# Keys' tiles that first hold x and the weights, and the first group's maxima among the projections

## The chip, the cores and the metric

The kernel runs on one core of one Trainium2 chip. The metric is the device time of one execution in microseconds (us); the time before is the median of three runs, 1368.82 us (1365.33 to 1370.16). A trace belongs to one profiled execution, which took 1366.65 us in all; the recorded span, from its first to its last instruction, is 1364.9 us.

## The reference, cut to what matters

Two independent computations, side by side in the output. A is a state-space convolution of u (2048 positions, 448 channels, 256 states); B is softmax attention with 16 heads of 28 on x (2048 x 448).

```python
qkv = (x @ wqkv).reshape(B, S, 3, H, Dh)      # q, k, v
scores = jnp.einsum("bhqd,bhkd->bhqk", q, k) * scale
p = softmax(scores, axis=-1)
o = jnp.einsum("bhqk,bhkd->bhqd", p, v)
b = o.transpose(...).reshape(B, S, D) @ wo

P = jnp.exp((A * dt[:, None])[:, :, None] * pos)       # pos = 0 .. L-1
K = 2.0 * jnp.einsum("dn,dnl->dl", C, P).real
y = irfft(rfft(u_t, 2 * L) * rfft(K, 2 * L))[:L] + u * D_skip
```

The softmax subtracts each query's maximum. What this kernel subtracts is a maximum over partly combined scores (below).

## The kernel before, in words

**Two phases.** The first phase ("p", from line 205) projects x to q, k and v and builds the *seeds* of the convolution's kernel K. The second ("a", from line 848) is a loop of 256 steps: 4 groups of 4 heads, 4 quarters of 512 queries (a pair of group and quarter is a *unit* u, 16 in all), 16 key tiles of 128. In it, work of the convolution is put between the attention's instructions by deques with due steps (`k_due`, `u_due`, `m_due`). In the second phase every instruction is kept in program order on its engine (`KEPT["a"]`); in the first none is, and the framework orders what is ready, earlier lines first.

**The first phase in stages.** `work` is a list of 48 jobs: for each quarter c of x, eight `qk_proj` (k and q of four groups) and four `v_proj`. Each job is 12 matmuls into one of three PSUM tiles, and an evacuation one job later: ACT writes the high part `th`, DVE the low part `tl` (two buffers of each), and SP writes both to DRAM (`k_d`, `q_d`; v goes through two staging tiles `vst` to `v_d`). The first job of a quarter also runs `transposes(c)`, the second loads the next quarter's x. For the first two quarters a k job also makes the difference of two halves of the keys and writes it to `kd_d`. In the last quarter the v jobs come before the q and k jobs.

The other strand is `seeds(o)`, eight of them, each a list of 13 steps on DVE, POOL and ACT, the steps of seed o at stages 4o to 4o + 12. The last two (`put_g`, `put_e`) write to DRAM. The scratch of `places()` is one of three `qhat` buffers. The loop over the 41 stages (line 515) runs, for stage t, as many jobs as are due (48 in the first 37 stages), then that stage's seed steps.

**What the change touches.** x lies in `y_p` (three half quarters, `xn`), v's weights in `y_p` (`vh`, `vl`), those of q and k in `w_p` (`wh`, `wl`). At stage 37 these pools close (`wst.close()`), and in the same memory `kd_p` (key differences, and the scratch `rl`) and `k0_p` (the four key tiles of a group, 128 x 2048 each, for even groups) are opened. Then SP is given `load_q(0)`, for each of four j `load_kd(0, j)` and `load_k(0, j)`, `load_q(1)` and four `load_v`. The keys of odd groups are in `kq_p`, a pool of the second phase. `load_k` reads one key tile in four DMAs.

**Maxima.** `max_mm(u, i, kc)` is one of 64 pieces of a unit's maxima: a matmul of 128 queries against 512 keys, and

- kc 0: against the key differences; ACT takes the Relu into `rl`;
- kc 1: against half of the keys of the first two quarters; DVE adds `rl` and reduces, in one instruction, and reads the result;
- kc 2 and 3: against the third and fourth quarter of the keys; DVE reduces.

So a step i needs DVE three times, and all four quarters of the keys. Unit 0's 16 steps follow the last stage, over five PSUM tiles (two `pt`, three `pm`). Then `max_join` reduces once more (`m<-mx` in the trace), `max_end` transposes, `max_put` writes the result into two rows of q's tile. The maxima of unit 1 and later run inside the loop, ahead of the scores by 16 key tiles and three (`LEAD`); three steps of unit 1 come just before the loop. After `sst.close()` the memory of the seeds goes to `kq_p` and `g_p`.

In the trace all engine instructions have the line of one helper (L73), so groups are told by tile names: `pm<-xh,wh` a projection of q or k, `pm<-vh,xh` one of v, `pt<-ident,xn` a transpose of x, `kdif`, `khat`, `qhat` a maximum, `pss` a score, `p` its exponential, `sg`, `tri`, `px`, `gz`, `x_e` the seeds (which also use `qhat` as scratch).

Of the kernel before, what the change touches and what calls it, by code (L numbers as in the profile page):

```python
# [1 line left out]

# [37 lines left out]
PS = 1  # L40
SGB, XB, XL = 2, 5, 4
K0, KP, KD, UP = 0, 3.5, 5, 3

N1 = 32
N2 = 64
# [43 lines left out]
def body(ctx, tc, a, out):  # L89
# [37 lines left out]

    q_p = pool(att, "q_p", side="right")
    v_p = pool(att, "v_p", side="right")

    def mm32(o, w, x_, start, stop, at=0):

# [4 lines left out]

    kt_g, kd_g, q_u, m_u, mh_u, o_u, rl_u = {}, {}, {}, {}, {}, {}, {}

    def load_k(g, j, p):  # L140
        t = p.tile([128, L], F32R, name="khat", bufs=HG)
        for r in range(4):
            nc.sync.dma_start(t[32 * r:32 * r + 32, :].bitcast(F32), k_d[g][r % 2, 32 * j:32 * j + 32, :])
        kt_g.setdefault(g, []).append(t)

    v_g = {}

# [4 lines left out]
    kd_p = [None]  # L152

    def load_kd(g, j):
        kd_g[g, j] = t = kd_p[0].tile([128, CQ], F32R, name=f"kdif{j}")
# [10 lines left out]
    def max_mm(u, i, kc, ps=w_tile):  # L166

        if i == 0 and kc == 0:
            m_u[u] = q_p.tile([128, HG, 4, 3], F32, name="mx", bufs=2)
        j, t = divmod(i, 4)  # L170
        pm = ps()
        q, kt = q_u[u][:, j, t * 128:(t + 1) * 128], kt_g[u // NQ][j]
        mx = m_u[u][:, j, t, max(kc - 1, 0):max(kc - 1, 0) + 1]
        if kc == 0:
            nc.tensor.matmul(pm, q, kd_g[u // NQ, j], start=True, stop=True)
            rl_u[u, i] = kd_p[0].tile([128, CQ], F32, name="rl", bufs=2)
# [26 lines left out]


    with ExitStack() as st:
        sst, xst, wst = ExitStack(), ExitStack(), ExitStack()
        t_p = pool(sst, "t_p")
        s_p = pool(sst, "s_p")
        x_p = pool(xst, "x_p")
        y_p = pool(wst, "y_p", side="right")  # L210
        w_p = pool(wst, "w_p", side="right")
# [6 lines left out]

        def load_x(c):
            xs = x[c * CQ:(c + 1) * CQ, :].rearrange("(t p) d -> p t d", p=128)  # L220
            for h in range(2):
                xns[c, h] = y_p.tile([128, 2, D], F32, name="xn", bufs=3)
                nc.sync.dma_start(xns[c, h], xs[:, 2 * h:2 * h + 2, :])

        load_x(0)
        wh = w_p.tile([CK, 2, NCK, H, 32], F32R, name="wh")
        wl = w_p.tile([CK, 2, NCK, H, 32], F32R, name="wl")
        vh = y_p.tile([CK, NCK, D], F32R, name="vh")
        vl = y_p.tile([CK, NCK, D], F32R, name="vl")
        for w in (wh, wl):  # L230
            nc.gpsimd.memset(w[:, :, :, :, DH:].bitcast(F32), 0.0)
        vst = [x_p.tile([128, H, 32], F32, name=f"vst{i}") for i in range(2)]
# [34 lines left out]
        for k in range(NCK):  # L267
            for s in (1, 0):
                src = wns[k][:, s, :].rearrange("p (h e) -> p h e", e=DH)
                nc.scalar.activation(wh[:, s, k, :, :DH], src, AF.Copy)  # L270
                nc.vector.tensor_tensor(wl[:, s, k, :, :DH], src, wh[:, s, k, :, :DH].bitcast(F32), ALU.subtract)
# [158 lines left out]
        def transposes(c):  # L430
            for k in range(NCK):
                pt = ps_t.tile([128, CQ], F32, name="pt")[:CK]
                for t in range(4):
                    nc.tensor.transpose(pt[:, t * 128:(t + 1) * 128], xns[c, t // 2][:, t % 2, k * CK:(k + 1) * CK], ident)
                xh[k] = x_p.tile([CK, CQ], F32R, name="xh", bufs=XB)
                xl[k] = x_p.tile([CK, CQ], F32R, name="xl", bufs=XL)
                nc.scalar.activation(xh[k], pt, AF.Copy)
                nc.vector.tensor_tensor(xl[k], pt, xh[k].bitcast(F32), ALU.subtract)

        def qk_proj(c, s, g):  # L440
            pp = w_tile()
            hs = slice(HG * g, HG * g + HG)
            n = 0
            for k in range(NCK):
                for w_, x_ in ((wh, xh), (wl, xh), (wh, xl)):
                    nc.tensor.matmul(pp, w_[:, s, k, hs, :].rearrange("p h e -> p (h e)"), x_[k],
                                     start=n == 0, stop=n == 3 * NCK - 1)
                    n += 1

            def evac():  # L450
                th = x_p.tile([128, CQ], F32R, name="th", bufs=2)
                tl = x_p.tile([128, CQ], F32R, name="tl", bufs=2)
                if s == 1:
                    nc.scalar.activation(th, pp, AF.Identity, bias=kones)
                    nc.vector.scalar_tensor_tensor(tl, pp, kones, th.bitcast(F32), op0=ALU.add, op1=ALU.subtract)
                else:
                    nc.scalar.activation(th, pp, AF.Copy)
                    nc.vector.tensor_tensor(tl, pp, th.bitcast(F32), ALU.subtract)
                if s == 1 and c < 2:
                    HC = CQ // 2  # L460
                    kb = y_p.tile([128, HC], F32, name="kb")
                    dh = y_p.tile([128, HC], F32R, name="dh")
                    dl = y_p.tile([128, HC], F32R, name="dl")
# [26 lines left out]
        for c in range(NQ):  # L490
            jobs = [lambda c=c, s=s, g=g: qk_proj(c, s, g) for g in range(G) for s in (1, 0)]
            v_jobs = [lambda c=c, t=t: v_proj(c, t) for t in range(4)]
            jobs = v_jobs + jobs if c == NQ - 1 else jobs + v_jobs
            jobs[0] = (lambda c, f: lambda: (transposes(c), f())[1])(c, jobs[0])
            if c + 1 < NQ:
                jobs[1] = (lambda c, f: lambda: (load_x(c + 1), f())[1])(c, jobs[1])
# [10 lines left out]
        def project():  # L507
# [4 lines left out]
            if e:  # L512
                pend.append(e)

        for t in range(n_stage):
            while work and n_work - len(work) < n_work * (t + 1) / PW:
                project()
            for f in slots[t]:
                f()
            if t + 1 == PW:  # L520
                project()
                wst.close()
                kd_p[0] = pool(att, "kd_p", side="right")
                k0_p = pool(k0_st, "k0_p", side="right")
                load_q(0)
                for j in range(HG):
                    load_kd(0, j)
# [24 lines left out]
    k_pools = [k0_p, kq_p]  # L552

    late = [False]

# [296 lines left out]
        for kc in range(4):  # L852
            max_mm(1, i, kc)

    import collections
# [124 lines left out]
    for s in range(NS):  # L980
# [18 lines left out]
        if sm < NS and sm % (NQ * NK) == 0 and sm:  # L999
            load_kd(sm // (NQ * NK), HG - 1)  # L1000
        if kt % 4 == 1 and u % NQ == 1 and u // NQ + 1 < G:
            load_k(u // NQ + 1, kt // 4, k_pools[(u // NQ + 1) % 2])
        if kt == 2:
            if u + 2 < NU:
                load_q(u + 2)
# [97 lines left out]
```

## Time and profile before

| | us |
|---|---|
| median of three runs | 1368.82 |
| profiled execution, in all | 1366.65 |
| its span | 1364.9 |
| PE busy | 1243.5 (91%) |
| DVE busy | 980.3 (72%) |
| ACT busy | 968.6 (71%) |
| POOL busy | 831.0 (61%) |
| mean granted clock of TensorE | 0.975 |
| moved by DMA | 205.37 MB, 150 GB/s over the span |

The profile's page gives the span in 40 slices; a digit is the busy share of an engine in tenths. Matmuls are pipelined: a projection's matmul is 0.4 us long, and the next begins 0.23 us after it. A view by windows gives the busy time of each engine between two times, with the granted clock and the DMA engines' share. The chain of waits follows the instruction that ended last back to what released it.

### The profile page before, as it was taken

What the parts mean: (1) busy time and instruction counts of PE and PEld (TensorE: products, weight loads), DVE (VectorE), ACT (ScalarE), POOL (GpSimd) and SP (SyncE); (2) the same over time, 40 slices, a digit from 0 to 9 for tenths busy, and PEclk for the clock granted to TensorE, in tenths of its full rate; (3) what the DMA queues carried; (4) which work ended last, traced back from release to release, by engine and by line L of the source; (5) the groups of instructions that cost most, each with busy time, mean ns of one, the idle gap of its engine ahead of it and who ended that gap; (6) DMA issues with size and microseconds to landing.
All of it is one profiled execution on the core that took longest, in us unless ns stands there. A gap on an engine that the chain in (4) does not pass through costs nothing.

```text
span 1364.9 us, 33230 instructions
## 1 busy us (share of the span) xinstructions
PE 1243.5 (91%) x12625; PEld 707.2 (52%) x12625; DVE 980.3 (72%) x2138; ACT 968.6 (71%) x2069; POOL 831.0 (61%) x705
## 2 busy tenths in 40 slices
PE   6978784799999999999999999999998999998997
PEld 4866662355555555555555555555555545544433
DVE  5778765877777777777788888887887766857311
ACT  4867662488888888888888888878786665655553
POOL 3576661187877877878878988888896111202221
PEclk9988896999999999999999999999999999999999
DMA  6775679726675546378533233632324544636476
GB/s 194 241 243 193 219 263 246 208 62 140 160 168 119 131 125 155 109 205 209 161 96 88 64 72 78 148 86 66 77 66 139 181 123 154 208 109 205 138 192 178
DMA packets 200729, 205.37 MB, mean 150 GB/s; under 512 B 96632, under 2 KB 159160, under 8 KB 198520
## 3 DMA queue, kind: packets, MB, share of 16 engines
q1 hardware_dynamic: 200568, 203.23, 53.5%
q8 instruction: 100, 1.64, 0.5%
q14 instruction: 61, 0.50, 0.1%
HBM read 120.73 MB, written 82.18 MB: 149 GB/s over the span
## 4 chain that ended last, share of the span: by engine, by line
PE 58%; DVE 16%; ACT 11%; POOL 5%; DMA 5%; issue 3%; SPq 0%; ACTq 0%; DVEq 0%; POOLq 0%
PE pm L73 34%; PE po L73 13%; PE pss L73 12%; ACT p L73 6%; DVE mx L73 3%; POOL qhat L73 3%; DVE g L73 2%; ACT rl L73 2%; DVE p L73 2%; DMA khat<-k 2%; DVE tri L73 1%; DVE pr L73 1%; DVE px L73 1%; POOL x_e L73 1%; DVE sg L73 1%
## 5 line engine op out<-in xcount | busy, mean ns | idle before, releaser
L73 ACT ACTIVATE p<-pss 128x512 f32<-128x512 f32 x1024 | 565.3, 608 | 137.0 <-PE pss L73 128.4
L73 PE MATMUL pss<-qhat,khat 128*128 128x512 f32 x1024 | 402.2, 399 | 3.5 <-ACT p L73 3.4
L73 DVE TENSOR_REDUCE mx<-pm 128x1 f32<-128x512 f32 x500 | 321.4, 683 | 104.6 <-PE pm L73 103.4
L73 PE MATMUL pm<-khat,qhat 128*128 128x512 f32 x749 | 329.7, 443 | 41.5 <-DVE mx L73 36.1
L73 POOL TENSOR_TENSOR e<-e,sdb 128x256 f32<-128x256 f32 x168 | 201.9, 1202 | 166.0 <-ACT e L73 157.0
L73 PE MATMUL po<-p,v 128*32 128x512 f32 x2048 | 271.8, 598 | 0.0
L73 POOL TENSOR_TENSOR e<-e,eu 128x256 f32<-128x256 f32 x168 | 248.5, 1479 | 13.2
L73 PEld LDWEIGHTS pm<-khat,qhat 128*128 128x128 f32 x749 | 141.0, 189 | 217.7 <-DVE mx L73 83.4
L73 PEld LDWEIGHTS pss<-qhat,khat 128*128 128x128 f32 x1024 | 190.6, 188 | 45.9 <-issue 11.1
L73 DVE CUSTOM_DVE_ANT_0 rl<-pm,rl 128x512 f32<-128x512 f32 x249 | 171.5, 689 | 47.3 <-ACT rl L73 44.2
L73 POOL TENSOR_TENSOR eu<-e,sdb 128x256 f32<-128x256 f32 x168 | 201.8, 1201 | 0.0
L73 DVE TENSOR_TENSOR g<-g,zg 128x128 f32<-128x128 f32 x392 | 162.9, 416 | 46.6 <-ACT zg L73 41.5
L73 ACT ACTIVATE rl<-pm 128x512 f32<-128x512 f32 x249 | 150.8, 606 | 24.9 <-PE pm L73 24.9
L73 POOL TENSOR_TENSOR p<-pr,pr 64x448 f32<-64x448 f32 x32 | 40.9, 1277 | 191.7 <-DVE pr L73 180.6
L73 PE MATMUL pm<-kdif,qhat 128*128 128x512 f32 x249 | 100.9, 405 | 2.4 <-DMA v<-v 1.3
L73 PEld LDWEIGHTS pm<-e,g 128*32 128x32 f32 x3584 | 63.0, 110 | 52.8 <-issue 30.9
L73 DVE TENSOR_TENSOR zg<-g,zg 128x128 f32<-128x128 f32 x224 | 87.5, 391 | 1.9
L73 PEld LDWEIGHTS po<-p,v 128*32 128x32 f32 x2048 | 56.5, 110 | 42.6 <-issue 37.9
L73 PE MATMUL pm<-e,g 128*32 128x64 f32 x3584 | 72.5, 220 | 0.0
L73 ACT ACTIVATE y<-pm 128x448 f32<-128x448 f32 x48 | 26.3, 548 | 63.5 <-PE pm L73 30.9
L73 PE MATMUL pm<-xh,wh 112*128 112x512 f32 x128 | 56.2, 443 | 11.2 <-DVE tl L73 5.1
L73 DVE TENSOR_TENSOR pr<-pm,ub 128x448 f32<-128x448 f32 x64 | 37.0, 619 | 32.7 <-PE pm L73 32.7
(137 smaller groups left out, 1555.4 us busy)
## 6 DMA issues: line engine op xcount, KB each, us to landing
sdb<-sd SPq DMA_DIRECT2D x56, 336.0 KB
qhat<-q SPq DMA_DIRECT2D x64, 256.0 KB
khat<-k SPq DMA_DIRECT2D x64, 256.0 KB
sd<-sg SPq DMA_DIRECT2D x8, 1456.0 KB
mw<-in_mw SPq DMA_DIRECT2D x16, 512.0 KB
sd<-qhat SPq DMA_DIRECT2D x8, 896.0 KB
yk<-yk SPq DMA_DIRECT2D x56, 128.0 KB
yu_d<-ub SPq DMA_DIRECT2D x64, 112.0 KB
```

Of the source, the lines that this page charges most:

```text
L73: i = f(*args, **kw)
```

## The change

1. The pools for x and the weights go. `kd_p` and two pools of key tiles, `k1_p` and `k0_p`, are open from the start. In `k0_p`, four tiles of 128 x 2048, lie x (a whole quarter in one tile) and `vh`, `vl`; in `k1_p` the two halves of `wh` and of `wl`, one tile each for q and k. v's staging tiles are two of the five `v` tiles. The scratch of the key difference is in two `rl` tiles. Keys of odd groups are loaded into `k1_p` later, and no longer lie in `kq_p`.
2. In the last quarter the first job (k of group 0) comes ahead of the four v jobs.
3. The loads of group 0 are given at stages: q of unit 0 at 24, key differences at 25, two key tiles at 28, two at 32, q of unit 1 and v at 39.
4. Unit 0's maxima are traced from stage 31 on, two steps i a stage, over two PSUM tiles (`pt`) while projections are left and over all five after. In each stage they come after the jobs and the seeds' steps of that stage.

```diff
+L0, L1, L2, L3, M0, MN = 24, 25, (28, 32), 39, 31, 2
...
+    kd_p = pool(att, "kd_p", side="right")
+    k1_p = pool(att, "k1_p", side="right")
+    k0_p = pool(k0_st, "k0_p", side="right")
+    k_pools = [k0_p, k1_p]
...
-    def load_k(g, j, p):
-        t = p.tile([128, L], F32R, name="khat", bufs=HG)
+    def k_tile(i):
+        return k_pools[i].tile([128, L], F32R, name="khat", bufs=HG)
+
+    def load_k(g, j, c=None):
+        if c in (None, 0):
+            kt_g.setdefault(g, []).append(k_tile(g % 2))
+        t, cs = kt_g[g][j], slice(0, L) if c is None else slice(c[0] * CQ, c[1] * CQ)
         for r in range(4):
...
         def load_x(c):
+            xns[c] = k_tile(0).bitcast(F32)[:, :4 * D].rearrange("p (t d) -> p t d", t=4)
             for h in range(2):
-                xns[c, h] = y_p.tile([128, 2, D], F32, name="xn", bufs=3)
...
+        vh, vl = (k_tile(0)[:CK, :NCK * D].rearrange("p (k d) -> p k d", k=NCK) for _ in range(2))
+        wh, wl = ([k_tile(1)[:CK].rearrange("p (k h e) -> p k h e", k=NCK, h=H) for _ in range(2)] for _ in range(2))
...
+        vst = [v_p.tile([128, NK // NQ, HG, 32], F32, name="v", bufs=5).rearrange("p t h e -> p (t h) e") for _ in range(2)]
...
+                    kb, dl = (kd_p.tile([128, CQ], F32, name="rl", bufs=2) for _ in range(2))
+                    kb, dh, dl = kb[:, :HC], kb[:, HC:].bitcast(F32R), dl[:, :HC].bitcast(F32R)
...
-            jobs = v_jobs + jobs if c == NQ - 1 else jobs + v_jobs
+            jobs = jobs[:1] + v_jobs + jobs[1:] if c == NQ - 1 else jobs + v_jobs
...
+        def maxima(i):
+            for kc in range(4):
+                ws = w2 if pend or work else w5
+                max_mm(0, i, kc, ws[n_max[0] % len(ws)])
+                n_max[0] += 1
+
+        firsts = collections.deque(lambda i=i: maxima(i) for i in range(16))
+        heads = {t: [lambda: firsts and firsts.popleft()()] * MN for t in range(M0, n_stage)}
+        for t, f in ((L0, lambda: load_q(0)), (L1, lambda: [load_kd(0, j) for j in range(HG)])):
+            heads.setdefault(t, []).insert(0, f)
+        for i in range(2):
+            heads.setdefault(L2[i], []).insert(i, lambda i=i: [load_k(0, 2 * i + j) for j in range(2)])
+        heads.setdefault(L3, []).insert(0, lambda: (load_q(1), [load_v(0, c) for c in range(NQ)]))
         for t in range(n_stage):
...
             for f in slots[t]:
                 f()
+            for f in heads.get(t, ()):
+                f()
             if t + 1 == PW:
                 project()
-                wst.close()
-                kd_p[0] = pool(att, "kd_p", side="right")
-                k0_p = pool(k0_st, "k0_p", side="right")
-                load_q(0)
-                for j in range(HG):
-                    load_kd(0, j)
-                    load_k(0, j, k0_p)
-                load_q(1)
-                for c in range(NQ):
-                    load_v(0, c)
-        more = [lambda: ps_t.tile([128, CQ], F32, name="pt")] * 2 + [w_tile] * 3
-        for i in range(16):
-            for kc in range(4):
-                max_mm(0, i, kc, more[(4 * i + kc) % 5])
```

More of the change, by code (lines that the diff above doesn't have):

```diff
@@ L1 @@
+import collections
 from contextlib import ExitStack
@@ L138, in body @@
     kt_g, kd_g, q_u, m_u, mh_u, o_u, rl_u = {}, {}, {}, {}, {}, {}, {}
-    def load_k(g, j, p):
-        t = p.tile([128, L], F32R, name="khat", bufs=HG)
+    def k_tile(i):
[4 more added lines that the diff above has]
+        t, cs = kt_g[g][j], slice(0, L) if c is None else slice(c[0] * CQ, c[1] * CQ)
         for r in range(4):
-            nc.sync.dma_start(t[32 * r:32 * r + 32, :].bitcast(F32), k_d[g][r % 2, 32 * j:32 * j + 32, :])
-        kt_g.setdefault(g, []).append(t)
+            nc.sync.dma_start(t[32 * r:32 * r + 32, cs].bitcast(F32), k_d[g][r % 2, 32 * j:32 * j + 32, cs])
     v_g = {}
@@ L150, in load_v @@
         nc.sync.dma_start(t.rearrange("p t h e -> p t (h e)"), v_d[c][:, g])
-    kd_p = [None]
     def load_kd(g, j):
-        kd_g[g, j] = t = kd_p[0].tile([128, CQ], F32R, name=f"kdif{j}")
+        kd_g[g, j] = t = kd_p.tile([128, CQ], F32R, name=f"kdif{j}")
         for r in range(4):
@@ L175, in max_mm @@
             nc.tensor.matmul(pm, q, kd_g[u // NQ, j], start=True, stop=True)
-            rl_u[u, i] = kd_p[0].tile([128, CQ], F32, name="rl", bufs=2)
+            rl_u[u, i] = kd_p.tile([128, CQ], F32, name="rl", bufs=2)
             nc.scalar.activation(rl_u[u, i], pm, AF.Relu)
@@ L205, in body @@
     with ExitStack() as st:
-        sst, xst, wst = ExitStack(), ExitStack(), ExitStack()
+        sst, xst = ExitStack(), ExitStack()
         t_p = pool(sst, "t_p")
@@ L209, in body @@
         x_p = pool(xst, "x_p")
-        y_p = pool(wst, "y_p", side="right")
-        w_p = pool(wst, "w_p", side="right")
         ps_w[0] = pool(st, "ps_w", 1, PSUM)
@@ L220, in load_x @@
             xs = x[c * CQ:(c + 1) * CQ, :].rearrange("(t p) d -> p t d", p=128)
+            xns[c] = k_tile(0).bitcast(F32)[:, :4 * D].rearrange("p (t d) -> p t d", t=4)
             for h in range(2):
-                xns[c, h] = y_p.tile([128, 2, D], F32, name="xn", bufs=3)
-                nc.sync.dma_start(xns[c, h], xs[:, 2 * h:2 * h + 2, :])
+                nc.sync.dma_start(xns[c][:, 2 * h:2 * h + 2, :], xs[:, 2 * h:2 * h + 2, :])
         load_x(0)
[L226 to L232, printed above, removed]
+        vh, vl = (k_tile(0)[:CK, :NCK * D].rearrange("p (k d) -> p k d", k=NCK) for _ in range(2))
+        wh, wl = ([k_tile(1)[:CK].rearrange("p (k h e) -> p k h e", k=NCK, h=H) for _ in range(2)] for _ in range(2))
+        for w in wh + wl:
+            nc.gpsimd.memset(w[:, :, :, DH:].bitcast(F32), 0.0)
+        vst = [v_p.tile([128, NK // NQ, HG, 32], F32, name="v", bufs=5).rearrange("p t h e -> p (t h) e") for _ in range(2)]
         for t in vst:
@@ L269, in body @@
                 src = wns[k][:, s, :].rearrange("p (h e) -> p h e", e=DH)
-                nc.scalar.activation(wh[:, s, k, :, :DH], src, AF.Copy)
-                nc.vector.tensor_tensor(wl[:, s, k, :, :DH], src, wh[:, s, k, :, :DH].bitcast(F32), ALU.subtract)
+                nc.scalar.activation(wh[s][:, k, :, :DH], src, AF.Copy)
+                nc.vector.tensor_tensor(wl[s][:, k, :, :DH], src, wh[s][:, k, :, :DH].bitcast(F32), ALU.subtract)
             nc.scalar.activation(vh[:, k, :], wns[k][:, 2, :], AF.Copy)
@@ L433, in transposes @@
                 for t in range(4):
-                    nc.tensor.transpose(pt[:, t * 128:(t + 1) * 128], xns[c, t // 2][:, t % 2, k * CK:(k + 1) * CK], ident)
+                    nc.tensor.transpose(pt[:, t * 128:(t + 1) * 128], xns[c][:, t, k * CK:(k + 1) * CK], ident)
                 xh[k] = x_p.tile([CK, CQ], F32R, name="xh", bufs=XB)
@@ L445, in qk_proj @@
                 for w_, x_ in ((wh, xh), (wl, xh), (wh, xl)):
-                    nc.tensor.matmul(pp, w_[:, s, k, hs, :].rearrange("p h e -> p (h e)"), x_[k],
+                    nc.tensor.matmul(pp, w_[s][:, k, hs, :].rearrange("p h e -> p (h e)"), x_[k],
                                      start=n == 0, stop=n == 3 * NCK - 1)
@@ L460, in evac @@
                     HC = CQ // 2
-                    kb = y_p.tile([128, HC], F32, name="kb")
-                    dh = y_p.tile([128, HC], F32R, name="dh")
-                    dl = y_p.tile([128, HC], F32R, name="dl")
+                    kb, dl = (kd_p.tile([128, CQ], F32, name="rl", bufs=2) for _ in range(2))
+                    kb, dh, dl = kb[:, :HC], kb[:, HC:].bitcast(F32R), dl[:, :HC].bitcast(F32R)
                     nc.scalar.activation(kb, pp[:, HC:], AF.Copy)
@@ L513, in project @@
                 pend.append(e)
+        w2 = [lambda: ps_t.tile([128, CQ], F32, name="pt")] * 2
+        w5 = w2 + [w_tile] * 3
+        n_max = [0]
+        def maxima(i):
[10 more added lines that the diff above has]
+        heads.setdefault(L3, []).insert(0, lambda: (load_q(1), [load_v(0, c) for c in range(NQ)]))
         for t in range(n_stage):
@@ L519, in body @@
                 f()
+            for f in heads.get(t, ()):
+                f()
             if t + 1 == PW:
                 project()
-                wst.close()
-                kd_p[0] = pool(att, "kd_p", side="right")
-                k0_p = pool(k0_st, "k0_p", side="right")
-                load_q(0)
-                for j in range(HG):
-                    load_kd(0, j)
-                    load_k(0, j, k0_p)
-                load_q(1)
-                for c in range(NQ):
-                    load_v(0, c)
+        while firsts:
+            firsts.popleft()()
         xst.close()
-        more = [lambda: ps_t.tile([128, CQ], F32, name="pt")] * 2 + [w_tile] * 3
-        for i in range(16):
-            for kc in range(4):
-                max_mm(0, i, kc, more[(4 * i + kc) % 5])
         max_join(0)
@@ L551, in body @@
     ps_w[0] = pool(ps_st, "ps_m", 1, PSUM)
-    k_pools = [k0_p, kq_p]
     late = [False]
@@ L853, in body @@
             max_mm(1, i, kc)
-    import collections
     urgent, back = collections.deque(), collections.deque()
@@ L1001, in body @@
         if kt % 4 == 1 and u % NQ == 1 and u // NQ + 1 < G:
-            load_k(u // NQ + 1, kt // 4, k_pools[(u // NQ + 1) % 2])
+            load_k(u // NQ + 1, kt // 4)
         if kt == 2:
```

## The prediction, made before the result was known

> **What bounds the kernel now.** I read three views: the page's rows by slices, the busy time by windows that I cut at the places where PE's row changes, and the chain of waits in order of time across those places.
>
> ```profile
> span 1364.9 us, 33230 instructions
> ...
> PE   6978784799999999999999999999998999998997
> ...
> DVE  5778765877777777777788888887887766857311
> ```
>
> A slice is 34 us. PE is at 9 from the ninth slice on; the only deep hole is before it. The windows show what lies there.
>
> ```profile
> 120.00:150.00 30.00, 24.49 (x102) 19.07 (x101) 26.03 (x47) 21.44 (x42) 19.46 (x25) 0.89 0.61 222
> ...
> 150.00:165.00 15.00, 9.34 (x43) 6.99 (x42) 9.50 (x19) 7.60 (x19) 11.87 (x16) 0.84 0.46 145
> 165.00:178.00 13.00, 13.00 (x58) 11.17 (x56) 11.29 (x18) 11.19 (x17) 6.33 (x7) 0.93 0.95 304
> 178.00:200.00 22.00, 20.03 (x82) 15.07 (x80) 15.36 (x30) 14.53 (x31) 14.20 (x20) 0.92 0.87 303
> 200.00:212.00 12.00, 0.00 (x0) 0.00 (x0) 7.73 (x19) 2.24 (x7) 5.42 (x9) 0.69 0.53 182
> 212.00:224.00 12.00, 1.62 (x3) 0.93 (x4) 0.00 (x0) 1.08 (x2) 4.18 (x5) 0.50 1.05 250
> 224.00:255.00 31.00, 24.86 (x62) 11.51 (x61) 29.21 (x65) 8.37 (x14) 0.00 (x0) 0.93 0.98 257
> 255.00:262.00 7.00, 6.13 (x14) 2.87 (x14) 5.34 (x14) 1.79 (x3) 0.00 (x0) 0.76 0.48 143
> ...
> 300.00:1250.00 950.00, 906.81 (x10453) 500.86 (x10446) 728.80 (x1638) 729.84 (x1602) 651.96 (x509) 1.00 0.49 128
> ```
>
> Columns: window, length, busy us of PE, weight loads, DVE, ACT, POOL, then the granted clock, the share of the DMA engines and GB/s. The attention loop (300 to 1250) has PE busy 906.81 of 950 us: it is bound by PE, and the change leaves its instructions and their order alone. From 178 to 255 three things follow one another: the last projections, a stretch in which POOL and the DMA queue finish (PE 1.62 us of 24), and unit 0's maxima, where DVE is busy 29.21 of 31.
>
> ```profile
> 152.28 0.45 PE L73 MATMUL pm<-vh,xh 112*128 112x448 f32 x1
> ...
> 172.56 0.39 PE L73 MATMUL pm<-xh,wh 112*128 112x512 f32 x1
> ...
> 199.23 0.40 PE L73 MATMUL pm<-xl,wh 112*128 112x512 f32 x1
> ...
> 219.17 0.79 PE L73 MATMUL pt<-kdif,qhat 128*128 128x512 f32 x1 [19.54 <-DMA kdif<-kd]
> ...
> 254.97 0.20 DVE L73 TENSOR_REDUCE m<-mx 128x16 f32<-128x48 f32 x1
> ...
> 262.29 0.40 PE L73 MATMUL pss<-qhat,khat 128*128 128x512 f32 x1
> ```
>
> PE's last projection starts at 199.23; its next instruction waits 19.54 us for a load. Maxima end at 254.97, and the attention's first scores (`pss`) come at 262.29, 7.3 us later. The chain says what the 20 us and more were:
>
> ```profile
> 212.18 4.81 DMA qhat<-q
> 217.01 5.53 DMA khat<-k
> 222.56 5.48 DMA khat<-k
> 228.06 5.48 DMA khat<-k
> 233.56 6.36 DMA khat<-k
> 239.94 6.82 DMA v<-v
> ```
>
> The loads queue one behind the other, 5.5 us for each key tile, because their memory is x's and the weights' until the last projection.
>
> **The change part by part.** The whole question is how early `m<-mx` (254.97) can come; what follows it is unchanged, so each us there is one of the span.
>
> *When the maxima can start.* The last k of group 0 moves from the fifth job of the fourth quarter to the first. So its matmuls run about where the first v job now starts (152.28) and not at 172.56. The first v job now waits on the quarter's transposes, and so will k; its write left SP 3.7 us after 172.56 in this trace, so I put it at about 167 (152 with the stalls of the transposes, some 10 us by the window 150 to 165 with PE 9.34 busy of 15, then 4 to 5 us).
>
> ```profile
> 176.27 0.34 SPq L73 DMA_DIRECT2D k<-th  x1
> ...
> 220.25 3.53 SPq L73 DMA_DIRECT2D khat<-k  x4
> ```
>
> Two key tiles at 5.5 us land at 178. The other two follow, two heads at a time, while the first are used.
>
> *What DVE has to do from 178.* Its present work: 15.36 + 7.73 = 23.1 us (windows 178 to 200 and 200 to 212). The maxima: 29.2 us (224 to 255). Sum 52.3. They no longer come one after the other, but not without gaps: the seeds make DVE wait for POOL (waits from 130 to 265: us in total, times, longest).
>
> ```profile
> DVE sg L73 <- POOL tri L73: 12.6, 3, 5.2
> ```
>
> The fullest 30 us of this stage (120 to 150) had DVE busy 26.03, or 0.87. I take this: 52.3 / 0.87 = 60.1, so 238. At 1.00 it is 230; at the 0.70 of 178 to 200 (15.36 of 22) it is 253. I choose 0.87 since independent reductions are what fills such gaps, and 120 to 150 had more independent work than 178 to 200.
>
> *The other engines.* PE: 20.0 us plus the maxima's 24.9 is 45, below DVE's 52. ACT: 16.8 us from 178 to 212 plus the sixteen `rl`, 8.4 us in the window of the maxima. POOL gets nothing. The half clock of 212 to 224 goes with PE's pause; DVE hides it already, so I count nothing, at best 1 us in 255 to 262 (clock 0.76).
>
> *The DMA engines* are the second bound. From 178 to 255 they are busy 0.87 x 22 + 0.53 x 12 + 1.05 x 12 + 0.98 x 31 = 68.5 us. Before 178 there is room for 0.54 x 15 + 0.05 x 13 = 8.8 us: group 0's q (4.8 us) and part of kdif go there, some 8 us in all. The key loads from 167 on only push other transfers. That leaves 60 us, so everything has landed at 238 and not before; only part of v isn't needed by then. Two resources full to the same minute get in each other's way: a put that waits behind a key tile (5.5 us) holds one of the two `th`/`tl` buffers, and with it a projection. I add 4 us, somewhat less than one key tile: maxima end at 242, bounds 0 and 11 (both halves' second tile). The Trainium skill, "DMA: Bandwidth & Descriptors", section Specifications, gives about 358 GB/s of HBM for a core; the 17.8 MB that the GB/s column leaves would then take 50 us, an estimate, the bound would be DVE's 238 alone, and the sum 4 us lower. This trace has 304 GB/s at a share of 0.95 with writes, but 257 at 0.98 while it reads the keys, so here the loads don't reach that figure.
>
> *SP* issues the same DMAs, earlier: 3.53 us for a key tile, 14 us for four. Its time there is mostly waiting, so nothing; what its order can do is the third rival.
>
> *Tiles.* x, both halves of the weights and v's staging sit in other memory with the same shapes and the same instructions: nothing. The key difference's scratch now holds two shared buffers; its next use waits for both writes, eight times in the first half, nothing to 5 us (eight times a 0.7 us wait), taken as nothing because PE had projections of other groups to run. Group 0's q holds one of the three `qhat` buffers from stage 24 on, which the seeds use as scratch: nothing if a scratch is written out within four stages (21 us at 199 / 37 a stage), else 896 KB at 250 GB/s, 3.6 us, up to three times. x is loaded a whole quarter ahead and not one and a half halves: minus 1 at best.
>
> *Sum.* 254.97 - 242 = 13. The profiled execution took 1366.65 us in all (span 1364.9), so 1353.7. The median of the runs shown is 2.2 above that execution: 1355.8. I say **1355**, with 1347 to 1362 for this case alone (fill 0.95 with no extra to 0.80 with 5 us).
>
> **The rivals.**
>
> *Everything packs.* DVE has no gap from 178 on and v lands last, unneeded: 230 to 232, 24 us less, 1344. For it: the maxima alone ran at 29.21 of 31. Against it: POOL's waits above, and the DMA engines' 238.
>
> *It packs no better than now, or the keys come late anyway.* With the fill of 178 to 200 the maxima end at 253, 2 us less. The same comes out if the key loads find no room (shares 0.95 and 0.87 from 165 to 200), land after 200 as today, and only the order changes. 1362 to 1368.
>
> *Slower: the seeds' tail sets the end.* Its rows now:
>
> ```profile
> 215.32 1.02 POOL L73 TENSOR_TENSOR qhat<-qhat,x_e 128x336 f32<-128x336 f32 x1
> ...
> 242.23 0.37 SPq L73 DMA_DIRECT2D sd<-sg  x1
> 243.39 0.37 SPq L73 DMA_DIRECT2D sd<-qhat  x1
> ...
> 257.27 1.04 SPq L73 DMA_DIRECT2D sdb<-sd  x2
> ```
>
> The last seed is done at 216.3, its 1456 + 896 KB (2.4 MB, 9.6 us at 250 GB/s) are written later, and all of it is hidden under the maxima, with 255.9 - 216.3 - 9.6 = 30 us to spare before the loop takes the seeds' memory. In the changed kernel maxima stand between the seeds' instructions on DVE, and puts behind key loads on SP. If all 29 us of maxima come ahead of the tail, and half of the loads' 27 us (22.9 for keys, 4.8 for q) as well, the tail is 43 us late, 13 beyond its room: 1379. It decides from 30 us on. For it: POOL and DVE alternate at the end, and SP keeps its order.
>
> ```profile
> SPq L73 <- ACT th L73: 17.2, 12, 3.4
> ```
>
> SP stood 17.2 us on `th` alone (waits of SP's own queue from 0 to 265), in front of whatever came next. The same page of the Trainium skill, section "Anatomy of one DMA", says that DMA engines do not wait on semaphores, the issuing sequencer does, before dispatch; the row agrees. Against it: the code puts each stage's seeds ahead of that stage's maxima, and the last eight maxima (two of four key tiles) can't come ahead of much.
>
> **How the numbers follow.** Forecast 0.54; packs fully 0.12; no gain 0.18; slower 0.16. A measurement of this kernel tells about 0.3%, or 4.1 us, from no change. Faster by more (under 1364.7): 0.54 + 0.12 + 0.04 of the third = 0.70. Within: the other 0.14 and 0.02 of the last, 0.16. Slower: 0.14. The range has to reach into the cases on both sides: 1344 takes in full packing, 1372 the third case and the near edge of the last; outside stay 0.06 below and 0.13 above.
>
> **What would show it.** In the changed profile: the first key loads issued between 160 and 175 (if after 200, the second rival); the first `mx` reductions at 175 to 185, mixed with `sg` and `tl`; no PE pause near 20 us; `m<-mx` at 235 to 248; the DMA share above 0.9 from 165 to 235; `pss` 7 us behind `m<-mx` (if more, the seeds' tail or a late v); the window from there to the end as long as now, 1102.6 us within 2. Wrong would be a loop that itself gets longer or shorter, or maxima that wait for PSUM (only two buffers while projections last) so that DVE idles on PE.

## The result, and the profile after

The changed kernel took **1390.04 us** (median of five runs, 1388.19 to 1390.37) against 1366.47 of the kernel before (five runs, 1365.33 to 1370.16): a ratio of 1.0159, 95% interval 1.0142 to 1.0176. It is slower by 1.6%; the forecast was 1355 with 0.70 on faster, and its range ended at 1372. The profiled execution has a span of 1387.4 us. All names of x and the weights are `khat` now, v's staging is `v`, every line is L75.

The page's slices after, PE and DVE, with the granted clock:

```profile
PE   6988558699999999999999999999998999998998
...
DVE  5787646577777877777777888788788766847411
...
PEclk9999777589999999999999999999999999999999
```

From the fifth slice to the eighth PE had 7, 8, 4 and 7; it has 5, 5, 8 and 6 now, at a clock that falls there. The same windows as before show where the time goes:

```profile
120.00:150.00 30.00, 24.72 (x111) 19.56 (x109) 22.77 (x43) 22.07 (x39) 15.90 (x18) 0.89 0.69 229
150.00:165.00 15.00, 6.15 (x21) 4.76 (x22) 11.81 (x24) 7.44 (x18) 12.03 (x15) 0.66 0.57 142
165.00:178.00 13.00, 3.42 (x11) 2.79 (x10) 1.95 (x4) 4.93 (x6) 7.40 (x8) 0.63 0.09 24
178.00:200.00 22.00, 15.75 (x65) 12.01 (x64) 11.31 (x23) 10.59 (x22) 6.39 (x10) 0.89 0.87 244
200.00:212.00 12.00, 5.24 (x8) 2.05 (x8) 5.87 (x12) 5.16 (x9) 7.24 (x8) 0.50 0.54 179
212.00:224.00 12.00, 10.73 (x22) 6.14 (x22) 6.01 (x12) 2.07 (x4) 0.00 (x0) 0.54 0.36 112
224.00:255.00 31.00, 24.50 (x70) 14.06 (x68) 23.86 (x52) 8.75 (x21) 8.88 (x14) 0.76 0.64 179
255.00:270.00 15.00, 11.62 (x25) 6.93 (x25) 8.66 (x18) 3.34 (x6) 0.00 (x0) 0.70 0.79 271
```

Read 165 to 178 first. Before, PE was busy 13.00 of 13 there and the DMA engines 0.95; now PE has 3.42, DVE 1.95, and the DMA engines 0.09. Nothing is full, so the engines wait for one another; such a chain of waits, from engine to engine, is called a ring below. From 200 to 224 it is so again: PE at half clock, DVE half busy, and from 212 to 224 POOL at 0.00 and the DMA engines at 0.36. DVE's busy time in the five windows from 178 to 270 adds up to 55.7 us in 92, a fill of 0.61.

Two places close the account, DVE's last maximum and the first score on PE:

```profile
270.03 0.20 DVE L75 TENSOR_REDUCE m<-mx 128x16 f32<-128x48 f32 x1
```

```profile
277.24 0.77 PE L75 MATMUL pm<-kdif,qhat 128*128 128x512 f32 x1 [6.59 <-DMA qhat<-q]
...
284.96 0.63 PE L75 MATMUL pss<-qhat,khat 128*128 128x512 f32 x1
```

`m<-mx` came at 254.97 and comes at 270.03: 15.1 us. `pss` followed 7.3 us behind it and follows 14.9 behind: 7.6 more, of which PE waits 6.59 for the q of unit 1, whose load is given at stage 39. That is 22.7 us. From `pss` to the end it is 1102.4 us (1102.6 before): the whole loss lies ahead of the loop.

**The first ring.** SP's own rows through the first stall, then DVE's and ACT's:

```profile
143.29 3.96 SPq L75 DMA_DIRECT2D qhat<-q  x4
147.63 0.56 SPq L75 DMA_DIRECT2D v<-v  x1
148.25 10.75 SPq L75 DMA_DIRECT2D kdif<-kd  x16
159.10 16.75 SPq L75 DMA_DIRECT2D v<-v  x2
175.94 0.88 SPq L75 DMA_DIRECT2D nat<-in_A_log_A_real  x1
...
181.60 0.57 SPq L75 DMA_DIRECT2D sd<-sg  x1
```

```profile
188.30 0.93 DVE L75 TENSOR_TENSOR sg<-tri 128x336 f32<-128x336 f32 x2 [21.28 <-DMA sd<-sg]
```

```profile
173.28 0.39 ACT L75 ACTIVATE gz<-gz 128x224 f32<-128x224 f32 x1 [4.82 <-POOL gz L75]
173.58 1.31 ACT L75 ACTIVATE tri<-tri,half_pi 128x1232 f32<-128x1232 f32 x1
174.79 0.52 ACT L75 ACTIVATE v<-pm 128x448 f32<-128x448 f32 x1
```

The new loads of q and of the key differences take SP 14.7 us of issuing, ahead of writes of v. The last of these has to wait for ACT's `v` at 174.79, which stands on ACT behind the seed's `gz`. Behind SP's wait stand the next seed's inputs (`nat`) and `sd<-sg`, the writing of a seed that DVE needs out of the way, since `sg` has two buffers. DVE stands 21.28 us. In the kernel before, the same two rows of SP came 24 and 17 us earlier:

```profile
151.56 1.39 SPq L73 DMA_DIRECT2D nat<-in_A_log_A_real  x1
...
164.83 0.59 SPq L73 DMA_DIRECT2D sd<-sg  x1
```

**The second ring** is at 197 to 227. ACT's rows, then SP's, then POOL's:

```profile
208.27 0.58 ACT L75 ACTIVATE rl<-pt 128x512 f32<-128x512 f32 x1
211.31 0.60 ACT L75 ACTIVATE rl<-pt 128x512 f32<-128x512 f32 x1 [2.46 <-PE pt L75]
214.37 0.60 ACT L75 ACTIVATE rl<-pt 128x512 f32<-128x512 f32 x1 [2.46 <-PE pt L75]
217.62 0.60 ACT L75 ACTIVATE rl<-pt 128x512 f32<-128x512 f32 x1 [2.65 <-PE pt L75]
218.11 0.98 ACT L75 ACTIVATE v<-pm 128x448 f32<-128x448 f32 x2
```

```profile
196.27 0.39 SPq L75 DMA_DIRECT2D sd<-sg  x1
218.68 1.20 SPq L75 DMA_DIRECT2D v<-v  x2
...
221.23 0.64 SPq L75 DMA_DIRECT2D sd<-qhat  x1
```

```profile
227.36 0.58 POOL L75 MEMSET qhat<- 128x112 f32 x2 [18.27 <-DMA sd<-qhat]
```

Maxima now stand among the projections in each engine's order. A step over two PSUM tiles takes 3.04 to 3.25 us (the distance of ACT's `rl`), and ACT's evacuation of v stands behind four of them. SP waits for it with the rest of its list, `sd<-qhat` among it, and POOL, which needs that seed scratch, waits 18.27 us until 227.36. PE's last projections end at 260.9, and not at 199.6. The half clock is the smaller part of the slow step: a matmul takes 0.80 us here, but where it takes 0.40 to 0.50, with `rl` at 231.24, 233.83 and 236.66, a step still takes 2.59 and 2.83.

The waits of SP's own queue from 130 to 290 (us in total, times, longest) say the same in one line each, first the changed kernel, then the kernel before, where v's staging is `vst`:

```profile
SPq L75 <- ACT v L75: 39.2, 3, 21.7
```

```profile
SPq L73 <- ACT vst L73: 12.8, 3, 7.8
```

### The profile page after: what moved, and what is told of

Its sections match the earlier page's. It is cut to its first block, busy times and chain, and to the rows that moved or that the text cites. A ratio compares the mean times of both kernels' runs of the same rounds, so it can differ in the third digit from the quotient of the medians.

```text
span 1387.4 us, 33226 instructions
## 1 busy us (share of the span) xinstructions
PE 1255.6 (90%) x12625; PEld 713.0 (51%) x12625; DVE 980.6 (71%) x2138; ACT 968.8 (70%) x2069; POOL 828.9 (60%) x707
## 4 chain that ended last, share of the span: by engine, by line
PE 61%; DVE 16%; ACT 11%; POOL 5%; issue 3%; DMA 3%; SPq 1%; ACTq 0%; DVEq 0%; POOLq 0%
PE pm L75 35%; PE po L75 13%; PE pss L75 12%; ACT p L75 6%; DVE mx L75 3%; POOL qhat L75 2%; DVE g L75 2%; ACT rl L75 2%; DVE p L75 2%; DVE pr L75 1%; DVE sg L75 1%; PE pt L75 1%; DVE px L75 1%; DVE tri L75 1%; SPq L75 1%
## 5 line engine op out<-in xcount | busy, mean ns | idle before, releaser
L75 ACT ACTIVATE p<-pss 128x512 f32<-128x512 f32 x1024 | 565.4, 609 | 137.7 <-PE pss L75 128.9
L75 PE MATMUL pss<-qhat,khat 128*128 128x512 f32 x1024 | 403.3, 400 | 2.5 <-ACT p L75 2.5
L75 DVE TENSOR_REDUCE mx<-pm 128x1 f32<-128x512 f32 x485 | 311.6, 684 | 104.6 <-PE pm L75 103.5
L75 PE MATMUL pm<-khat,qhat 128*128 128x512 f32 x728 | 322.5, 446 | 41.7 <-DVE mx L75 35.8
L75 POOL TENSOR_TENSOR e<-e,sdb 128x256 f32<-128x256 f32 x168 | 201.8, 1201 | 158.3 <-ACT e L75 149.3
L75 PE MATMUL po<-p,v 128*32 128x512 f32 x2048 | 271.8, 598 | 0.0
L75 POOL TENSOR_TENSOR e<-e,eu 128x256 f32<-128x256 f32 x168 | 248.2, 1478 | 13.2
L75 PEld LDWEIGHTS pm<-khat,qhat 128*128 128x128 f32 x728 | 138.1, 190 | 213.8 <-DVE mx L75 79.3
L75 PEld LDWEIGHTS pss<-qhat,khat 128*128 128x128 f32 x1024 | 191.1, 189 | 46.0 <-issue 11.1
L75 DVE CUSTOM_DVE_ANT_0 rl<-pm,rl 128x512 f32<-128x512 f32 x243 | 167.5, 689 | 54.1 <-ACT rl L75 51.7
L75 POOL TENSOR_TENSOR eu<-e,sdb 128x256 f32<-128x256 f32 x168 | 201.7, 1200 | 0.0
L75 DVE TENSOR_TENSOR g<-g,zg 128x128 f32<-128x128 f32 x392 | 163.0, 416 | 46.3 <-ACT zg L75 41.3
L75 ACT ACTIVATE rl<-pm 128x512 f32<-128x512 f32 (+1 forms) x250 | 149.9, 599 | 30.8 <-PE pm L75 28.2
L75 POOL TENSOR_TENSOR p<-pr,pr 64x448 f32<-64x448 f32 x32 | 40.9, 1277 | 191.6 <-DVE pr L75 180.5
L75 PE MATMUL pm<-xh,khat 112*128 112x512 f32 x256 | 93.0, 444 | 14.5 <-DVE tl L75 6.4
L75 PE MATMUL pm<-kdif,qhat 128*128 128x512 f32 x242 | 97.3, 402 | 7.4 <-DMA qhat<-q 6.6
L75 PEld LDWEIGHTS pm<-e,g 128*32 128x32 f32 x3584 | 63.0, 110 | 52.8 <-issue 31.6
L75 DVE TENSOR_TENSOR zg<-g,zg 128x128 f32<-128x128 f32 x224 | 87.5, 391 | 1.9
L75 PEld LDWEIGHTS po<-p,v 128*32 128x32 f32 x2048 | 56.5, 110 | 42.7 <-issue 38.0
L75 PE MATMUL pm<-e,g 128*32 128x64 f32 x3584 | 72.5, 220 | 0.0
L75 ACT ACTIVATE y<-pm 128x448 f32<-128x448 f32 x48 | 26.3, 548 | 62.7 <-PE pm L75 30.5
L75 PEld LDWEIGHTS pm<-xh,khat 112*128 112x128 f32 x256 | 53.0, 212 | 29.2 <-DVE tl L75 7.7
```

What stands on the lines that cost most here:

```text
L75: i = f(*args, **kw)
```

## The experiments

The theory after the first look: **SP's order** (loads put early stand ahead of writes that others need) and **maxima over two PSUM tiles ahead of the projections**. Rivals: the new tiles; the order of k and v; the loads' traffic and the buffers that they hold. Each edit is in the line of constants (L0 the stage of q, L1 of the key differences, L2 of the key tiles, L3 of q of unit 1 and v, M0 the first stage of maxima, 99 for after the stages, MN steps a stage) unless a diff says more. The changed kernel has `24, 25, (28, 32), 39, 31, 2`. "v first" is this edit, which undoes part 2 of the change:

```diff
-            jobs = jobs[:1] + v_jobs + jobs[1:] if c == NQ - 1 else jobs + v_jobs
+            jobs = v_jobs + jobs if c == NQ - 1 else jobs + v_jobs
```

All were timed beside the kernel before (medians 1366.8 to 1367.4); the number behind each time is the ratio to it, and brackets hold its 95% interval.

### Tiles alone: e1_tiles_only, e5_load_order

e1: `36, 36, (36, 36), 36, 99, 2`, v first.

> Only the tiles are moved: loads of group 0 in one go at stage 36, all of unit 0's maxima after the stages, v jobs first in the last quarter, as before. If the tiles cost nothing (both theories), 1362 to 1371, within 0.3% of before. If x, weights and staging in the keys' and v's tiles are themselves the loss, 1380 or more.

1392.08 us, 1.0176 [1.0152, 1.0199]: a miss, through the edit. The loads came out in reverse, keys and differences ahead of q, so PE's first maximum waited 47.1 us for `qhat<-q`. e5 gives the loads in the order of the kernel before, behind the last job:

```diff
+        def load_all():
+            load_q(0)
+            for j in range(HG):
+                load_kd(0, j)
+                load_k(0, j)
+            load_q(1)
+            for c in range(NQ):
+                load_v(0, c)
```

> The tiles alone once more, with group 0's loads in the order of before (q, then key difference and key tile by turns, q of unit 1, v); in the run before, key differences came behind all key tiles and the first maximum waited 47 us. If that order was all of its loss: 1362 to 1371. If the shared tiles cost something themselves: 1380 or more.

1364.97 us, 0.9989 [0.9977, 1.0001]. The tiles cost nothing that these runs can tell.

### One part back at a time: e2, e3, e4, e7, e9

e2, maxima last: `24, 25, (28, 32), 39, 99, 2`.

> As after, but unit 0's maxima after all stages; the loads stay at stages 24 to 39 and k of group 0 stays ahead of v. Theory 1 (the early loads close a ring SP, v staging, ACT, SP, and cost the 20 us of DVE idle near 166 to 188): still 1380 to 1392. Theory 2 (maxima on two PSUM tiles stand in PE's order ahead of the last projections): the loss goes, 1345 to 1366, since the keys are there when the maxima start.

1378.95 us, 1.0085 [1.0068, 1.0102], outside both ranges: neither theory alone is the loss. Maxima among the projections cost 11.1 of the 23.6 us between the two medians; the rest is still there, and so is DVE's wait on `sd<-sg` (21.8 us).

e3, q and differences later: `30, 30, (28, 32), 39, 31, 2`. e7, earlier: `20, 21, (28, 32), 39, 31, 2`.

> As after, but q of unit 0 and the key differences are loaded at stage 30, not 24 and 25; key tiles and maxima as in after. Theory 1: SP has 20 DMAs fewer ahead of the third quarter's v writes, the ring opens, 1355 to 1372. Theory 2: the maxima stand where they stood, 1383 to 1392.

> As after, but q of unit 0 and the key differences are loaded at stages 20 and 21, between the v writes of the second and the third quarter. Theory 1: the third quarter's v writes are free of them, 1370 to 1382, the rest being the maxima. Theory 2: 1385 to 1392.

1379.96 us, 1.0092 [1.0073, 1.0112], and 1380.99 us, 1.0103 [1.0087, 1.0120]. Both are 9 to 10 us faster than the changed kernel and still slower than before by 1%; e3 lies outside both of its ranges. One window of each, first e3, then e7:

```profile
178.00:200.00 22.00, 14.61 (x40) 11.03 (x41) 11.53 (x25) 11.66 (x22) 7.65 (x13) 0.57 0.26 68
```

```profile
120.00:150.00 30.00, 13.65 (x52) 10.72 (x51) 20.23 (x34) 16.82 (x27) 21.14 (x25) 0.66 0.54 152
```

The stall moves with the loads. In e7 it comes earlier (PE 13.65 of 30). In e3 it comes later (the DMA engines at 0.26), and there it stands behind the key tiles, which SP now issues at 165.85 and not at 188.93; e3 left them at their early stages, and e13 below shows what they cost alone.

e4, v first, with the keys and the maxima a little later: `24, 25, (32, 33), 39, 34, 2`.

> As after, but the v jobs come first in the last quarter again; so the key tiles are loaded at stages 32 and 33 and the maxima begin at 34, q and key differences stay at 24 and 25. Theory 1: q and key differences are still ahead of the third quarter's v writes on SP, 1378 to 1392. Theory 2: fewer maxima lie between projections (stages 34 to 36 in place of 31 to 36), about half of the loss, 1374 to 1382. If k ahead of v is itself the loss, 1350 to 1368.

1378.12 us, 1.0076 [1.0053, 1.0099]. With v first it is still slower than before by 11 us, so k ahead of v isn't the whole cause. This run also moves the key tiles and the maxima, and its time lies in both theories' ranges; e16 below undoes the order of k and v alone.

e9, five PSUM tiles for the maxima from the start:

```diff
-                ws = w2 if pend or work else w5
+                ws = w5
```

> As after, but the maxima use all five PSUM tiles (two pt, three pm) from the start, also while projections are left. Theory 2a (two tiles: matmul and reduction take turns, 3 us a step in place of 1.8): 1375 to 1384. Theory 2b (any maxima in front of the last projections in PE's order, whatever the tiles; the pm tiles are also the projections'): 1385 to 1400.

1380.89 us, 1.0100 [1.0070, 1.0130]: 9.2 us of the 11.1 come back, with some 4 us of doubt. So most of what the maxima cost hangs on the two tiles. Pace and place aren't separated: with five tiles the framework also put v's evacuation on ACT at 209.86, behind one `rl` and not four, so SP went on 8 us earlier (210.42, and 218.68 in the changed kernel).

### Another queue for one write: e6_sg_act_queue

```diff
-            put_g = lambda: nc.sync.dma_start(sd_d[o][:, :, F_G:]...
+            put_g = lambda: nc.scalar.dma_start(sd_d[o][:, :, F_G:]...
```

> As after, but the seeds' larger write (sg) is issued on ACT's queue, not on SP's. Theory 1 (SP's order: the write of sg stands behind v's writes, DVE stands 21 us for the sg buffer): DVE's wait goes to under 5 us and the time falls by 8 to 20, 1370 to 1382. If the wait at 166 to 188 is hidden by other late work (theory 2, maxima ahead of projections set the end): 1385 to 1392.

1381.60 us, 1.0102 [1.0085, 1.0120]. DVE's wait of 21 us is gone, 8.4 us of the time; POOL then waits 18.5 us for `sd<-qhat`, which still stands in SP's list.

### Late loads: e8, e10, e11, e12, e15, e16

e8: `33, 34, (33, 35), 39, 99, 2`. e10: the same with maxima from stage 35, e11: from 37, four a stage.

> As after, but q and key differences at stages 33 and 34, key tiles at 33 and 35, all maxima behind the stages: both suspects are taken away (loads past the third quarter's v writes, no maxima ahead of projections) and the keys are still early. Both theories together: 1345 to 1366, at or below before. If the two leave a loss above 1375, something third is at work.

> As the kernel with late loads and maxima last (1359.8), but the maxima traced from stage 35 on, two steps a stage, so some lie ahead of the last projections. Theory 2: 1365 to 1376. If maxima among projections cost nothing once the loads are late: 1350 to 1361.

> As the same kernel, but the maxima traced at stages 37 to 40, four steps a stage: behind all projections, among the seeds' last steps. Theory 2 speaks only of projections, so 1354 to 1362. If the seeds' tail is held up by them as projections are: 1363 to 1372.

e8 1359.83 us, 0.9942 [0.9925, 0.9958]; e10 1361.30, 0.9962 [0.9949, 0.9974] (in PE's order no maximum got ahead of the last projection); e11 1358.17, 0.9936 [0.9911, 0.9962]. Between e2 and e8 only the loads move, and that is 19.1 us: the same tiles, jobs and bytes are 0.9% slower than before with the loads early, and 0.6% faster with the loads late.

e12: `32, 32, (33, 35), 39, 99, 2`; e15: e12's loads with e11's maxima; e16: e12 with v first.

> As the same kernel, but q and key differences both at stage 32, ahead of the key tiles and still behind the last quarter's v writes. In that kernel the first maximum waited 9.6 us for q, so 5 to 10 us less if nothing else moves: 1350 to 1356. If those 20 DMAs hold back q's and k's writes of the last projections: 1358 to 1368.

> q and key differences at 32, key tiles at 33 and 35, maxima at stages 37 to 40, four steps a stage: the two changes that were each about 2 us faster than late loads with maxima last. If they add: 1354 to 1357. If the DMA engines set the end of both: 1357 to 1360.

> q and key differences at 32, key tiles at 33 and 35, maxima last, and the v jobs first again in the last quarter: k's place undone alone (1358.0 with k first). If k ahead of v gains time for the key tiles: 1362 to 1368. If it doesn't matter by then: 1355 to 1361. If it costs (PE stands 10 us for an evacuation of v at 165 to 178 in that kernel): 1345 to 1354.

**e12 1357.96 us, 0.9929 [0.9901, 0.9958]**, the lowest median (e8, e11, e15 and e17 lie within 2 us of it), faster than both kernels; e15 1359.40, 0.9947 [0.9928, 0.9966], so the two don't add; e16 1361.27, 0.9959 [0.9943, 0.9975]: k ahead of v may be worth 3 us (the two intervals overlap). e12's windows, and its end on DVE:

```profile
178.00:200.00 22.00, 16.37 (x61) 12.56 (x61) 17.28 (x33) 12.28 (x24) 13.41 (x18) 0.89 0.86 236
200.00:212.00 12.00, 5.96 (x17) 4.22 (x17) 7.01 (x18) 3.25 (x8) 6.94 (x8) 0.62 1.02 275
212.00:224.00 12.00, 9.38 (x19) 4.76 (x19) 8.97 (x18) 3.48 (x6) 0.00 (x0) 0.72 1.04 287
224.00:255.00 31.00, 25.31 (x61) 11.65 (x60) 27.89 (x63) 9.12 (x15) 0.00 (x0) 0.89 0.84 253
```

```profile
245.70 0.20 DVE L75 TENSOR_REDUCE m<-mx 128x16 f32<-128x48 f32 x1
```

The pause of PE at 200 to 224 is partly filled (15.34 us of 24, and 1.62 before) and the DMA engines are full there; the maxima end at 245.70, 9.3 us earlier than in the kernel before. They don't lie among the projections: but for one matmul at 197.64 they begin at 210.12, behind the last projection.

### Which load: e13_keys_early, e14_q_kdif_early

e8 with one load early: the keys (`33, 34, (28, 32), 39, 99, 2`), or q and differences (`24, 25, (33, 35), 39, 99, 2`).

> Maxima last; key tiles early (28 and 32, as in after), q and key differences late (33 and 34). If the 20 DMAs of q and key differences ahead of v's writes are the loss: 1354 to 1364. If the key tiles ahead of v's writes are: 1374 to 1384.

> Maxima last; q and key differences early (24 and 25, as in after), key tiles late (33 and 35). If q and key differences are the loss: 1374 to 1384. If the key tiles are: 1354 to 1364. If each is half: about 1369 in both of these runs.

1376.60 us, 1.0074 [1.0051, 1.0096], and 1368.78, 1.0009 [0.9999, 1.0020]. Against e8 the keys alone cost 16.8 us, q and differences alone 9.0; both together (e2) 19.1. They don't add (25.8 against 19.1); a stall that one makes seems to hide part of the other's. What the keys do is seen in SP's waits for `v` from 130 to 290, e13 first, then e8:

```profile
SPq L75 <- ACT v L75: 28.6, 3, 24.2
```

```profile
SPq L75 <- ACT v L75: 7.3, 4, 3.9
```

### The loads out of SP's order: e17, e18

All this would also fit the loads' traffic, or the `qhat` buffer that q holds. Against traffic stands e14's own row for the first stall, with the DMA engines at 0.09:

```profile
165.00:178.00 13.00, 3.87 (x11) 2.94 (x10) 1.67 (x4) 4.65 (x6) 7.39 (x8) 0.50 0.09 24
```

So e14 and the changed kernel were run with the same 20 early loads issued by POOL:

```diff
-            nc.sync.dma_start(t[32 * r:32 * r + 32].bitcast(F32), kd_d[g]...
+            (nc.gpsimd if g == 0 else nc.sync).dma_start(t[32 * r:32 * r + 32].bitcast(F32), kd_d[g]...
-            nc.sync.dma_start(t[32 * r:32 * r + 32].bitcast(F32), q_d[g]...
+            (nc.gpsimd if u == 0 else nc.sync).dma_start(t[32 * r:32 * r + 32].bitcast(F32), q_d[g]...
```

> The kernel with q and the key differences loaded at stages 24 and 25, late keys and maxima last (1368.8 us, against 1359.8 with those loads late), with these 20 loads issued by POOL and not by SP. If the 9 us are SP's order (SP holds the next inputs and the second writing of sg behind 15 us of issuing and the writes of v behind them), they come back: 1357 to 1362, the inputs of the next seed issued near 147 us and not 176, sd<-sg near 156 and not 181, no wait of 20 us of DVE on sd<-sg. Rival: it is the transfers' traffic, the third qhat buffer held from stage 24, or POOL's own time to issue: 1367 to 1372.

> The changed kernel as it is, with the same 20 loads (q of unit 0, key differences of group 0) issued by POOL. If SP's order is the ring, DVE's 21 us wait goes and about half of the loss with it: 1375 to 1381 (the keys at stages 28 and 32 still stand in SP's order, and the maxima among projections still cost their 9 to 11 us). Rival, loss by traffic or by a held qhat buffer: 1386 to 1392.

e17: **1359.73 us, 0.9945 [0.9929, 0.9962]**. The 9 us are back in full (e14 1368.78, e8 1359.83), although POOL's order let the loads go even earlier, and q still holds its buffer from 141 on. POOL's rows, then SP's:

```profile
73.07 0.66 POOL L75 DMA_DIRECT2D kdif<-kd  x1
...
141.16 0.59 POOL L75 DMA_DIRECT2D qhat<-q  x1
143.52 1.66 POOL L75 DMA_DIRECT2D qhat<-q  x3
```

```profile
149.93 2.14 SPq L75 DMA_DIRECT2D nat<-in_A_log_A_real  x1
...
160.23 0.57 SPq L75 DMA_DIRECT2D sd<-sg  x1
```

The next inputs leave at 149.93 and the seed at 160.23; in e14 it was 175.67 and 182.01. For q and the differences the held buffer is ruled out, which e17 holds as long, and by the row above so is the traffic. It is the order of SP's list: the loads that stood in it, and where the framework then puts the rest.

e18: 1383.87 us, 1.0121 [1.0106, 1.0136]: 6.2 us back where 9 to 15 were expected, a miss by 3. The first stall of DVE went, and the second ring seems to have taken part of it back. SP's rows and a window:

```profile
167.56 4.88 SPq L75 DMA_DIRECT2D khat<-k  x8
173.09 1.70 SPq L75 DMA_DIRECT2D v<-v  x2
175.47 0.39 SPq L75 DMA_DIRECT2D sd<-sg  x1
210.58 1.20 SPq L75 DMA_DIRECT2D v<-v  x2
```

```profile
200.00:212.00 12.00, 9.89 (x15) 4.28 (x16) 7.40 (x15) 3.42 (x7) 0.66 (x1) 0.50 0.02 5
```

The key tiles leave 21 us earlier, the maxima start earlier, and SP stands from 175.9 to 210.58 for the evacuation of v behind them, with the DMA engines at 0.02 from 200 to 212.

## Why the prediction was wrong, point by point

- **"SP issues the same DMAs, earlier ... so nothing"** is the step that failed. Its order is what counts, and the forecast gave it no price. An early load in SP's list stands ahead of other writes, and those wait for ACT, with the seeds' writes behind them and DVE or POOL behind these. The loads early and not late are worth 19.1 us (e2 against e8); for q and the key differences, 9.0 us alone, e17 shows that it is SP's list. For the key tiles, 16.8 us alone, it is argued from SP's wait for `v` (28.6 us in e13, 7.3 in e8); they weren't tried on another queue.
- **DVE's sum and its fill.** 52.3 us of work looks nearly right (55.7 in the windows above), in part by luck: 10 us of DVE's work had slipped from before 178 to behind it, and 7 us more was done ahead of 120. The fill was 0.61 and not 0.87. "Independent reductions" fill gaps only if they can run: DVE stood behind its own `sg` for 21.28 us, with the reductions behind it. And over two PSUM tiles a step takes 3.04 to 3.25 us, where the 29.21 us of the maxima gave 1.8. That case stood under "what would be wrong" without a price; five tiles gave 9.2 us back (e9).
- **The start at 178.** Key loads were to leave between 160 and 175. They left at 188.93, behind the same waits, so the maxima had no second piece to work on before 197.58.
- **DMA as second bound.** 60 us of transfers from 178 on assumed a queue that always has something to send. Shares of 0.09 and 0.36 show that it hadn't. The end it gave (238, then 242) is near what e12 reaches with full DMA engines, 245.70 (a share of 0.95 from 178 to there). The forecast took 257 GB/s, at a share of 0.98, for what key loads reach; in e14 it was 344 from 217 to 226, at a share of 1.04, with a seed's write among them.
- **"7 us behind m<-mx"** for `pss`: 14.9, for a late q of unit 1, as the text had allowed for v.
- **"The seeds' tail sets the end"**, the slower rival with 0.16, named SP's order and maxima ahead of the seeds, and those are the causes. (Its 1379 is the profiled execution plus 13; on the forecast's base, 2.2 us higher, it is 1382.) Its place was wrong: it priced a delay only where the tail runs out of its 30 us, while the seeds and projections in the middle had no room. In the trace the tail is late by just that room (POOL's last seed instruction ends at 246.9, and at 216.3 before), but in front of `pss` PE stood for maxima and for q, and from `pss` on the time is the same: the tail didn't set the end. The Trainium skill, "DMA: Bandwidth & Descriptors", section "Anatomy of one DMA", says that the sequencer that issues does the waiting; SP's 39.2 us on ACT's `v` agree. The prediction had quoted the rule and applied it only to that tail.
- **Right:** tiles at nothing (e5), the loop unchanged (1102.4 us), and, roughly, the size of the gain once nothing is held up: 9.3 us of the forecast's 13 (e12, with DVE at 0.80 from 178 on). The way to it was another: e12's maxima run behind the projections, and its key tiles leave earlier than before and later than in the changed kernel. No run gained by maxima that lie among projections.

The same page of the Trainium skill, section "Rules for kernel authors", says that spreading DMAs over SP, ACT and GpSimd doesn't help bandwidth and only saves the sequencer's issue time. No run here tests the bandwidth. On the second point e17 differs: 14.7 us of issuing left SP, and with it the stalls behind it, DVE's 22.8 us on `sd<-sg` in e14 among them.

What stays open: the framework orders the first phase anew with each edit, so a single us of e10 to e18 belongs to no one part; the key tiles weren't issued by another engine; how the 13 and 14 us that e3 and e7 still lose divide between loads and maxima wasn't measured; a third `sg` buffer wasn't tried.

## What to carry to other kernels

A load that is moved earlier moves ahead of everything that its queue had in front of it: write down what stands behind it in that queue, how many buffers that work has, and who stops when they are full. If a stretch shows no full engine and an idle DMA, look at the issuing queue's own waits. Work put in front of another stage's work holds it up for as long as it takes there, so look at the pace it will have: here five PSUM tiles in place of two gave back 9.2 of 11.1 us.

## What the runs showed of the hardware

- SP's time to issue the same loads isn't fixed. Eight loads of key tiles took 3.68 us in e8 and 8.90 in e14; four of q took 1.87 us before and 3.96 in the changed kernel. Full DMA engines alone don't explain it: e14's other eight took 3.70 us with the engines at 1.05 (206.7 to 210.4). During the 8.90 us SP's waits name DMAs that it had just given, 3.9 us for `sd<-sg` and 2.2 for key loads. For q's 3.96 us no wait is named, so that stays open.
- PE's granted clock falls to 0.50 in windows in which PE is busy 82% (e18, 200 to 212: 9.89 of 12), and one matmul takes 0.80 us there and not 0.40. The 15 matmuls of that window would be 6 us at most at 0.40, so a PE that waits for PSUM between matmuls looks busier than its work.
